# Two places for the first scores, and fewer idle products, in a fused attention and gated MLP kernel

## The chip, the cores and the metric
The kernel runs on one core of a Trainium2 chip. The metric is the device time of one execution in microseconds. The kernel before took 822.72 us (median of 3 runs, 822.22 to 823.4).

PE is the matmul engine, with PEld for its weight loads; DVE, ACT and POOL are the vector, scalar and general engines; SP issues the transfers (DMA). PSUM is the memory into which PE writes, in 8 banks of 512 fp32 columns.

## What is computed
Windowed attention over 8 batches of 8 heads, 576 positions of 64 dims, and then a gated two-layer product over the 4608 tokens:

```python
def _attn_ref(q, k, v):
    B, H, S, D = q.shape                      # 8, 8, 576, 64
    scores = np.matmul(q, k.transpose(0, 1, 3, 2)) / np.sqrt(D)
    rel = pos[:, None] - pos[None, :]
    mask_plain = (rel >= 0) & (rel < 32)
    mask_dil = (rel >= 0) & (rel < 128) & (rel % 4 == 0)    # heads 4 to 7
    scores = np.where(masks, scores, -1e9)
    attn = softmax(scores)
    return np.matmul(attn, v)

def _moe_ref(x, w_in, w_out):                 # x: 4608 x 512, d_ff 2048
    h = x @ w_in
    g = h * (1.0 / (1.0 + np.exp(-1.702 * h)))
    return g @ w_out
```

## The kernel before
Everything is one straight program without loops on the chip. A planner (class `Plan`) takes every step with its cost on each engine that could do it, its urgency, and named keys that it reads and writes. `placed` picks step after step by planned start time and appends it to one order; each engine then runs its own steps in that order, first in, first out. The keys only decide this order. The waits on the chip are put in by the framework from what the instructions really touch.

Two head pairs make a unit: pair k of batch 0 (k = 0 to 3) holds heads 2k and 2k + 1; pairs 2 and 3 are dilated. The text calls the steps of the first batch, "the first entry", s, p and d with the number of the pair:

- s0 to s3, `scores(k)`: a mask product by the identity (line 478) and then 42 tiled products of q and k (line 490, 32 rows of scores each, 64 columns). An fp32 product stands in the trace as two matmuls with two weight loads, hence x84. The result lies in the tile `sp` of two banks, one for each head; there is one such place, key "sp".
- the softmax of k: DVE takes the maximum (line 510) and subtracts it (line 353, pr<-sp) straight out of `sp`; then ACT's exp, DVE's sum and reciprocal, POOL's two multiplications, and DVE's transposes into `ct` (line 695), which has two buffers by turns.
- p0 to p3, `first_product(k)`, line 576: 46 or, dilated, 40 tiled products of v and `ct` into the tile `first_x` of four banks. Pair k takes columns 0 to 143 (k even) or 144 to 287 (k odd) of each bank. The step writes the keys FOUR (acc0 to acc3), all four banks.
- d0 to d3, `drain_x(k)`: ACT copies x into `xs` as the high parts (line 346, xs<-first_x), DVE subtracts to get the low parts (line 353, xs<-first_x,xs), and ACT or DVE copies the last 64 columns (arena<-first_x). These read FOUR, so p of the next pair waits for d of this one.

p0 also waits for s3 (key scores3). Urgency is k - 1e5 for s and p, k for the softmax, 0 for the products of the main block. The main block (class `Group`, `up`, from line 851 on) is x by w_in: for each of 16 columns f four steps c of three 512-column products, step c needing the high and low parts of x for pair c. Then comes the gate (lines 871 and 872), and the second product (lines 800 to 804). Weights arrive packed and are decoded on ACT, DVE and POOL (`decode`, from line 363 on) in the order of use.

Where PE's next step is planned later than PE is free, `placed` fills in idle products (lines 183 to 193), until 60 us of plan and until the third main column begins: `size` is the planned time of one, and a gap gets as many whole ones as fit after 0.5 us is taken off. Before 25 us of plan it may first put in small ones (line 188), just enough to take the count of instructions over the next multiple of 256 after 193. `fetched` is the planner's account of instructions that are loaded in blocks of 256; `count=` of a step is the number of its instructions. The idle products are issued by `warm` (line 1252 on): small ones of 16 columns at line 1262, others of 512 columns at line 1258.

Of the kernel before, what the change touches and what calls it, by code (L numbers as in the profile page):

```python
# [7 lines left out]
F32 = mybir.dt.float32  # L8
# [39 lines left out]
class Plan:  # L48
# [62 lines left out]
    def placed(self, warm_until, soon, late=None):  # L111
# [41 lines left out]
        while any(open_):  # L153
# [28 lines left out]
            cost = abs(ops[i][0][e])  # L182
            if e == PE and when < warm_until:

                at, size = max(free[e], 1.0), 0.26 if when > 8.0 else 0.44
                if when < SHORT and blocks[-1] < when - 0.3:

                    small = min((193 + 256 * (len(blocks) - 1) - issued[0]) // 4 + 1, int((when - at - 0.1) / 0.045))
                    order.extend([(None, e)] * small)
                    at = fetched(4 * small, at, small * 0.045)  # L190
                idle = max(0, int((when - max(at, 1.5) - 0.5) / size))
                fetched(2 * idle, at, idle * size)
                order.extend([(-1, e)] * idle)
            order.append((i, e))
            starts[i] = when
            if e == PE:
# [20 lines left out]
def tile_windowed_attention_then_gated_mlp(  # L217
# [87 lines left out]

    mask, plain = fixed([P, QT, W], BF16, "mask"), fixed([P, QT, W], BF16, "plain")
    ident = fixed([P, P], BF16, "ident")
    ones = fixed([P, 32], F32, "ones")
    V.memset(ones, 1.0)
    for p in sets[0:2]:  # L310
        V.memset(p[:, :, :, W], 1.0e-9)
    V.memset(ident, 1.0)
# [157 lines left out]

    def scores(k):
        u = pairs[k]
        u["sp"] = bank([P, 2, GT], "sp", f"sp_{k}")
        u["all"] = u["sp"][:, :, 0:QT * W].rearrange("p a (t w) -> p a t w", t=QT)
        u["box"] = [u["all"][:, a] for a in range(2)]
        if masked(k):
            for a in range(2):
                T.matmul(u["box"][a], ident, plain if not dilated(k) else classes if k < NC else mask, start=True,
                         stop=False, skip_group_check=True)
        for t in range(QT):  # L480
            for a, g in [(a, g) for a in range(2) for g in range(4 if k < NC or t < QT - 1 else 2)]:
                rows = slice(D * a, D * a + D)
                dst = u["box"][a][32 * g:32 * g + 32, t]
                at = ROW * g + 32 * t if k < NC else HALF * (g // 2) + W * t + 32 * (g % 2)

                spans = [(0, W, at - 32)]
                if at + 32 > S:
                    spans = [(0, S + 32 - at, at - 32), (S + 32 - at, at + 32 - S, 0)]
                for w, n, first in spans:
                    T.matmul(dst[:, w:w + n], u["qk"][rows, at:at + 32], u["qk"][rows, S + first:S + first + n],  # L490
                             start=not masked(k), stop=True, tile_position=(D * a, 32 * g), skip_group_check=True)

    def add_mask(k, urgency):
        u, pr, mine = pairs[k], prs[turn(k)], mask if dilated(k) else plain
        for n, tiles, cost in ((P, slice(0, QT - 1), 0.62), (D, slice(QT - 1, QT), 0.22)):
# [2 lines left out]
                mine[0:n, None, tiles].broadcast_to([n, 2, tiles.stop - tiles.start, W]), ALU.add),  # L498
                ("sp",), (f"pr{turn(k)}",))

    def exponentials(k, urgency):
        u, y = pairs[k], turn(k)
        pr, mx = prs[y], mxs[y]
        PR, MX = f"pr{y}", f"mx{y}"
        held = ("sp",) if masked(k) else ()

        def sp():
            return u["all"] if masked(k) else pr

        add({DVE: 0.80}, urgency, lambda e: V.tensor_reduce(out=mx, in_=sp(), axis=AX.X, op=ALU.max),  # L510
            held or (PR,), (MX,))
        add({DVE: 0.80 if masked(k) else -0.80}, urgency, lambda e: pair(
            e, pr, sp(), mx[:, :, :, None].broadcast_to([P, 2, QT, W]), ALU.subtract), (*held, MX), (PR,))
        add({ACT: 0.75}, urgency, lambda e: A.activation(prs[y], prs[y], AF.Exp, scale=0.125), (), (PR,))
# [98 lines left out]
    def drain_x(k, urgency):  # L613
# [24 lines left out]
                     (GT - HALF, lambda y: y[:, HALF:], lambda: x(1, 0, GT - HALF), 1)]  # L638
            rests = [(lambda y: y, lambda: x(2, 0, LT), 1)]
        if b == 0:  # L640

            if dilated(k):
                mains = [(GT, lambda x: x.rearrange("p (i r) -> p r i", r=4), lambda: u["x"][:, :, 0:P])]
                rests = [(lambda x: x.rearrange("p (i r) -> p r i", r=4), lambda: u["x"][:, :, P:])]
# [3 lines left out]
                rests = [(lambda x: x, lambda: u["x"][:, 3, GT - 3 * ROW:])]  # L648
            for n, (size, part, src) in enumerate(mains):
                add({ACT: 0.12 + size * (0.0019 if dilated(k) else 0.00094)}, urgency, lambda e, part=part, src=src: copy(  # L650
                    e, part(xh[:, c]), src()), FOUR, (f"xh{c}.{n}",))
                add({DVE: 0.08 + size / (490 if dilated(k) else 820)}, urgency, lambda e, part=part, src=src: pair(
                    e, part(xl[:, c]), src(), part(f32(xh[:, c])), ALU.subtract), (*FOUR, f"xh{c}.{n}"), (f"xl{c}.{n}",))
            for n, (part, src) in enumerate(rests):
                add({ACT: 0.22, DVE: 0.2}, urgency, lambda e, part=part, src=src: copy(
                    e, part(rests_x[:, 1, c]), src()), FOUR, (f"xr1{c}.{n}",))
            store_rest(b, c, urgency)
            return
        banks = ("av", "left") if k < INNER else ("sp", "sp")
# [23 lines left out]
    def first_attention(k):  # L683
# [1 line left out]

        load_qk(k)
        load_v(k)
        add({PE: 1.5 if k else 2.3}, k - 1.0e5, lambda e: scores(k), (lots(k)[0],), ("sp", f"scores{k}"), count=180)
        softmax(k, k)

    def first_transposed(k):
# [5 lines left out]
    def first_multiplied(k):  # L697


        y = turn(k)  # L700
        add({PE: 1.4}, k - 1.0e5, lambda e: first_product(k), (lots(k)[1], f"ct{y}.0", f"ct{y}.1", f"scores{NC - 1}"),
            FOUR, count=184)
        drain_x(k, k)

    def attention(k, urgency):
# [547 lines left out]
    def warm(i):  # L1253
        if 2 not in main[0].hps:
            if "idle" not in misc:
                misc["idle"] = bank([P, GT], "av", "idle")
            if i is not None:
                T.matmul(misc["idle"], ident, ident[:, None, :].broadcast_to([P, GT // P, P]), start=True, stop=True)
                return
            n = misc["small"] = misc.get("small", 0) + 1  # L1260
            col = 32 * (n % 4)
# [51 lines left out]
```

## Time and profile before

| | |
|---|---|
| median of 3 runs | 822.72 us |
| span of the profiled execution | 820.7 us |
| difference of the two, around the span | 2.0 us |
| PE busy, share of the span | 809.3 us, 99% |
| DVE, ACT, POOL busy | 669.0, 518.0, 328.4 us |
| chain of work that ended last | PE 97%, DMA 1%, DVE 1% |
| first of the 512-column main products | 25.62 us |
| p3 ends | 32.76 us |

Busy time is the union of an engine's instructions; matmul ends are modelled, so a busy PE is not PE at its peak, and the rate is read from starts. A row of the timeline merges instructions of one kind that follow each other: start, length, engine, line, operation, tiles written <- read, shape, count, and in brackets how long the engine stood idle before and what released it. "issue" there is a wait that no semaphore explains. The granted clock of PE is 1.00 at 2.4 GHz and 0.50 at 1.2 GHz. Ahead of the first change of clock that the profile recorded it prints 1.00 too; there the length of an idle product tells more.

### The profile page before, as it was taken

What the parts mean: (1) busy time and instruction counts of PE and PEld (TensorE: products, weight loads), DVE (VectorE), ACT (ScalarE), POOL (GpSimd) and SP (SyncE); (2) the same over time, 40 slices, a digit from 0 to 9 for tenths busy, and PEclk for the clock granted to TensorE, in tenths of its full rate; (3) what the DMA queues carried; (4) which work ended last, traced back from release to release, by engine and by line L of the source; (5) the groups of instructions that cost most, each with busy time, mean ns of one, the idle gap of its engine ahead of it and who ended that gap; (6) DMA issues with size and microseconds to landing.
All of it is one profiled execution on the core that took longest, in us unless ns stands there. A gap on an engine that the chain in (4) does not pass through costs nothing.

```text
span 820.7 us, 18890 instructions
## 1 busy us (share of the span) xinstructions
PE 809.3 (99%) x7279; PEld 653.4 (80%) x7279; DVE 669.0 (82%) x1081; ACT 518.0 (63%) x988; POOL 328.4 (40%) x294
## 2 busy tenths in 40 slices
PE   7999999999999999999999999999999999999997
PEld 4677878888887888778888888888888888888886
DVE  6898988888888876899889899996679885867575
ACT  7898986767577766786866654545456534544340
POOL 3442325455556553244345445531215332112251
PEclk9999999999999999999999999999999999999999
DMA  9577658899758657797788777775565658674545
GB/s 354 186 249 212 175 161 296 287 318 303 241 176 271 223 180 243 252 307 234 235 236 264 253 254 249 234 256 183 179 207 189 198 189 275 201 226 157 180 153 181
DMA packets 109610, 188.13 MB, mean 229 GB/s; under 512 B 26448, under 2 KB 55376, under 8 KB 109520
## 3 DMA queue, kind: packets, MB, share of 16 engines
q1 hardware_dynamic: 109376, 186.78, 70.2%
q8 instruction: 58, 0.95, 0.5%
q14 instruction: 32, 0.26, 0.1%
q10 hardware_dynamic: 144, 0.13, 0.0%
HBM read 140.64 MB, written 45.09 MB: 226 GB/s over the span
## 4 chain that ended last, share of the span: by engine, by line
PE 97%; DMA 1%; DVE 1%; issue 0%; ACT 0%; SPq 0%; DVEq 0%
PE hp_m L863 16%; PE up_p L1006 10%; PE up_r L1006 9%; PE up_q L1006 9%; PE acc_m L800 5%; PE second_p_Q L1121 5%; PE second_q_Q L1121 5%; PE acc_m L804 5%; PE acc_m L801 5%; PE second_r_Q L1121 5%; PE sp L490 4%; PE second_q_Z L1121 3%; PE second_r_Z L1121 3%; PE second_R L1121 3%; PE second_p_Z L1121 3%; PE av L608 2%
## 5 line engine op out<-in xcount | busy, mean ns | idle before, releaser
L353 POOL TENSOR_TENSOR arena<-arena 128x256 f32<-128x256 f32 (+3 forms) x94 | 100.7, 1083 | 97.8 <-DVE wi_last_units L353 21.6
L863 PE MATMUL hp_m<-xs,wi_kept 128*128 128x512 f32 x504 | 127.7, 396 | 1.2 <-DVE arena L872 0.9
L863 PEld LDWEIGHTS hp_m<-xs,wi_kept 128*128 128x128 f32 x504 | 92.9, 188 | 22.8 <-DVE arena L872 1.9
L353 POOL TENSOR_TENSOR wo_kept<-arena,wo_kept 128x512 fp32r<-128x512 f32 x41 | 56.9, 1395 | 131.5 <-ACT wo_kept L346 84.9
L346 ACT ACTIVATE wo_kept<-arena 128x512 fp32r<-128x512 f32 x111 | 69.2, 630 | 40.7 <-PE second_r_Q L1121 10.9
L1006 PE MATMUL up_r<-wi_kept,xs 128*128 128x512 f32 x336 | 85.3, 389 | 0.0
L1006 PE MATMUL up_p<-wi_kept,xs 128*128 128x512 f32 x336 | 84.2, 394 | 0.2 <-DVE arena L353 0.2
L1006 PE MATMUL up_q<-wi_kept,xs 128*128 128x512 f32 x336 | 83.4, 389 | 0.0
L1006 PEld LDWEIGHTS up_p<-wi_kept,xs 128*128 128x128 f32 x336 | 62.1, 188 | 14.7 <-DVE arena L353 0.9
L1006 PEld LDWEIGHTS up_q<-wi_kept,xs 128*128 128x128 f32 x336 | 63.0, 188 | 13.3 <-DVE arena L1028 0.3
L1006 PEld LDWEIGHTS up_r<-wi_kept,xs 128*128 128x128 f32 x336 | 63.1, 188 | 13.1
L353 DVE TENSOR_TENSOR wo_kept<-arena,wo_kept 128x512 fp32r<-128x512 f32 x80 | 61.1, 775 | 5.1 <-ACT wo_kept L346 4.7
L346 ACT ACTIVATE bt<-ct 32x256 f32<-32x256 f32 (+1 forms) x130 | 56.6, 435 | 11.7 <-DVE ct L534 6.0
L353 POOL TENSOR_TENSOR pr<-pr,sm 128x320 f32<-128x320 f32 x52 | 43.7, 856 | 48.5 <-DVE sm L518 43.5
L800 PE MATMUL acc_m<-gh,wo_kept 128*128 128x512 f32 x156 | 61.5, 394 | 0.0
L353 POOL TENSOR_TENSOR wo_kept<-wi_last_units,wo_kept 128x512 fp32r<-128x512 f32 x22 | 29.9, 1361 | 78.3 <-ACT wo_kept L346 72.3
L353 DVE TENSOR_TENSOR arena<-arena 128x512 f32<-128x512 f32 (+1 forms) x75 | 59.1, 797 | 2.7 <-ACT arena L346 1.8
L801 PE MATMUL acc_m<-gh,wo_kept 128*128 128x512 f32 x156 | 60.8, 390 | 0.0
L1027 ACT ACTIVATE arena<-arena 128x512 f32<-128x512 f32 x60 | 37.4, 628 | 33.4 <-DVE arena L353 27.2
L1028 DVE SCALAR_TENSOR_TENSOR arena<-arena 128x512 f32<-128x512 f32 x60 | 49.8, 837 | 1.7 <-ACT arena L1027 1.3
L346 ACT ACTIVATE gh<-arena 128x512 fp32r<-128x512 f32 x57 | 36.0, 631 | 17.5 <-DVE arena L872 5.8
L353 DVE TENSOR_TENSOR gl<-arena,gh 128x512 fp32r<-128x512 f32 x53 | 41.3, 779 | 6.5 <-ACT gh L346 3.2
(267 smaller groups left out, 1824.7 us busy)
## 6 DMA issues: line engine op xcount, KB each, us to landing
xs<-sums SPq DMA_DIRECT2D x168, 256.0 KB, 3.3
out_weights<-sums_o SPq DMA_DIRECT2D x63, 512.0 KB, 3.5
qk<-qk_dram SPq DMA_DIRECT2D x29, 576.0 KB, 4.4
xs<-sums_o SPq DMA_DIRECT2D x21, 512.0 KB, 3.8
v<-vp_dram SPq DMA_DIRECT2D x28, 320.0 KB, 4.1
sums_o<-arena SPq DMA_DIRECT2D x32, 256.0 KB, 3.2
sums<-arena SPq DMA_DIRECT2D x32, 256.0 KB, 2.9
arena<-wi_dram SPq DMA_DIRECT2D x15, 512.0 KB, 4.7
```

The costliest lines, as they stand in the source:

```text
L346: A.activation(dst, src, AF.Copy, scale=scale)
L353: (V if e == DVE else G).tensor_tensor(out=dst, in0=a, in1=b, op=op)
L490: T.matmul(dst[:, w:w + n], u["qk"][rows, at:at + 32], u["qk"][rows, S + first:S + first + n], start=not masked(k), stop=True, tile_positi ...
L608: T.matmul(u["x"][i][rows, at:at + last - first], u["v"][keys, a, m], bt[keys, m, a, first:last], start=(bank_, a) not in begun, stop=True ...
L800: T.matmul(self.acc[j], w[:, 0, cols], high, start=f == 0, stop=False)
L801: T.matmul(self.acc[j], w[:, 1, cols], high, start=False, stop=False)
L804: T.matmul(self.acc[j], w[:, 0, P * j:P * j + P], low, start=False, stop=f == NF - 1)
L863: T.matmul(hps[f], wi(f)[:, st, cols], mv[:, c], start=c == 0 and k == 0, stop=c == NC - 1 and k == 2)
L1006: T.matmul(self.banks[place], xs[:, slot, at:at + P], wi_kept[:, 2 * a + c, mv], start=fresh and c == 0 and k == 0, stop=c == 1 and k == 2 ...
L1027: add({ACT: 0.60}, -10.0, lambda e: A.activation(unit(tmp), src(), AF.Tanh, scale=0.851), need, own(tmp))
L1028: add({DVE: -0.70 if need[0][0] == "A" else 0.70}, -10.0, lambda e: V.scalar_tensor_tensor(out=unit(dst), in0=unit(tmp), scalar=1.0, in1=s ...
L1121: T.matmul(self.second[key], w[:, st, cols], mv, start=fresh and y == 0 and k == 0, stop=y == 1 and k == 2, skip_group_check=True)
```

## The change
- The scores of pairs 1 and 3 go to columns 192 to 511 of the first two banks of `first_x`; those of 0 and 2 stay in `sp`. Their keys are "x1" and "sp" (`home`).
- The products write the key "x0" or "x1" by turns in place of FOUR, which they now only read; the drains read both. So in the planner p of the next pair no longer waits for d of this one; p1 and p3 wait for the softmax of 3 and for d1.
- Pairs 0 to 3 leave out the second of two spans at the last tile (columns of keys that wrap round): 40 products in place of 42.
- `count` is set to the real numbers: 164 for scores, 184 or 160 for products.
- After 8 us of plan an idle product is now an fp32 one by `wide`, a new 128 x 128 tile of ones, planned at 1.3 us and four instructions; up to 8 us it stays as it was. `wide` is filled by POOL at the start.

```diff
-                at, size = max(free[e], 1.0), 0.26 if when > 8.0 else 0.44
+                at, size, n = max(free[e], 1.0), 0.44, 2
+                if 8.0 < when:
+                    size, n = 1.3, 4
...
-                fetched(2 * idle, at, idle * size)
-                order.extend([(-1, e)] * idle)
+                fetched(n * idle, at, idle * size)
+                order.extend([(-n // 2, e)] * idle)
...
-    ones = fixed([P, 32], F32, "ones")
+    ones, wide = fixed([P, 32], F32, "ones"), fixed([P, P], F32, "wide")
     V.memset(ones, 1.0)
+    G.memset(wide, 1.0)
...
-        u["sp"] = bank([P, 2, GT], "sp", f"sp_{k}")
+        u["sp"] = first_x[:, 0:2, GT - QT * W:] if k in (1, 3) else bank([P, 2, GT], "sp", f"sp_{k}")
...
-                    spans = [(0, S + 32 - at, at - 32), (S + 32 - at, at + 32 - S, 0)]
+                    spans = [(0, S + 32 - at, at - 32)] if k < NC else [
+                        (0, S + 32 - at, at - 32), (S + 32 - at, at + 32 - S, 0)]
...
+    def home(k):
+        return "x1" if k in (1, 3) else "sp"
+
...
-        held = ("sp",) if masked(k) else ()
+        held = (home(k),) if masked(k) else ()
...
+            X = f"x{k % 2}"
...
-                    e, part(xh[:, c]), src()), FOUR, (f"xh{c}.{n}",))
+                    e, part(xh[:, c]), src()), (X, *FOUR), (f"xh{c}.{n}",))
...
-        add({PE: 1.5 if k else 2.3}, k - 1.0e5, lambda e: scores(k), (lots(k)[0],), ("sp", f"scores{k}"), count=180)
+        add({PE: 1.5 if k else 2.3}, k - 1.0e5, lambda e: scores(k), (lots(k)[0],), (home(k), f"scores{k}"), count=164)
...
-        add({PE: 1.4}, k - 1.0e5, lambda e: first_product(k), (lots(k)[1], f"ct{y}.0", f"ct{y}.1", f"scores{NC - 1}"),
-            FOUR, count=184)
+        add({PE: 1.4}, k - 1.0e5, lambda e: first_product(k), (lots(k)[1], f"ct{y}.0", f"ct{y}.1", f"scores{NC - 1}", *FOUR),
+            (f"x{k % 2}",), count=160 if dilated(k) else 184)
...
-                T.matmul(misc["idle"], ident, ident[:, None, :].broadcast_to([P, GT // P, P]), start=True, stop=True)
+                a = ident if i == -1 else wide
+                T.matmul(misc["idle"], a, a[:, None, :].broadcast_to([P, GT // P, P]), start=True, stop=True)
```

## Rows read from the trace of the kernel before

**Rows 1.** The page, busy us of each engine (share of the span, instructions).

```profile
PE 809.3 (99%) x7279; PEld 653.4 (80%) x7279; DVE 669.0 (82%) x1081; ACT 518.0 (63%) x988; POOL 328.4 (40%) x294
```

**Rows 2.** PE's waits (total, times, longest); chain of waits; PE's timeline from 38 us.

```profile
PE hp_m L863 <- DVE arena L872: 0.9, 1, 0.9
...
63.79 2.72 PE hp_m L863 x12
...
37.80 1.99 PE L863 MATMUL hp_m<-xs,wi_kept 128*128 128x512 f32 x5
```

**Rows 3.** PE's timeline from 0 to 60 us.

```profile
13.97 1.13 PE L490 MATMUL sp<-arena 64*32 64x64 f32 x84
15.03 2.33 PE L1258 MATMUL idle<-ident 128*128 128x512 bf16 x10
...
17.56 0.86 PE L490 MATMUL sp<-arena 64*32 64x64 f32 x65
20.25 0.37 PE L490 MATMUL sp<-arena 64*32 64x64 f32 x19 [1.83 <-issue]
20.55 1.49 PE L576 MATMUL first_x<-ct,v 32*64 32x32 f32 x92
21.96 2.63 PE L1258 MATMUL idle<-ident 128*128 128x512 bf16 x6
24.53 1.16 PE L576 MATMUL first_x<-ct,arena 32*64 32x32 f32 x92
25.62 1.65 PE L863 MATMUL hp_m<-xs,wi_kept 128*128 128x512 f32 x6
...
27.43 1.42 PE L576 MATMUL first_x<-ct,arena 32*64 32x64 f32 x80
...
31.68 1.08 PE L576 MATMUL first_x<-ct,arena 32*64 32x64 f32 x80
32.69 7.11 PE L863 MATMUL hp_m<-xs,wi_kept 128*128 128x512 f32 x27
```

**Rows 4.** SP's timeline: the issues of the second qk and of a weight.

```profile
2.19 0.43 SPq L435 DMA_DIRECT2D arena<-qk_dram  x1
...
4.13 0.45 SPq L392 DMA_DIRECT2D bt<-wi_dram  x1
```

**Rows 5.** The same two DMA issues: count, size, us from issue to landing.

```profile
arena<-qk_dram SPq DMA_DIRECT2D x1, 576.0 KB, 7.1
...
bt<-wi_dram SPq DMA_DIRECT2D x1, 512.0 KB, 10.8
```

**Rows 6.** Windows: busy by engine in order of the page, clock, DMA share, GB/s.

```profile
16.00:17.00 1.00, 1.00 (x7) 0.41 (x6) 0.82 (x2) 1.00 (x2) 1.00 (x2) 1.00 1.05 425
22.00:23.00 1.00, 1.00 (x5) 0.39 (x4) 0.92 (x3) 0.91 (x4) 0.01 (x1) 0.50 0.43 157
```

**Rows 7.** DMA queues from 17 to 18 us (packets, MB, share); PEld's timeline.

```profile
q8 instruction: 1, 0.02, 6.9%
...
28.18 0.58 PEld L576 LDWEIGHTS first_x<-ct,arena 32*64 32x64 f32 x41 [0.18 <-issue]
```

**Rows 8.** DVE's and ACT's timelines: maximum and subtraction of s3, drains.

```profile
20.72 0.82 DVE L510 TENSOR_REDUCE mx<-sp 128x10 f32<-128x640 f32 x1 [1.22 <-PE sp L490]
21.58 0.82 DVE L353 TENSOR_TENSOR pr<-sp,mx 128x640 f32<-128x640 f32 x1
22.90 0.76 DVE L353 TENSOR_TENSOR xs<-first_x,xs 128x432 fp32r<-128x432 f32 x2
34.08 0.28 DVE L348 COPY arena<-first_x 128x64 f32<-128x64 f32 x1 [0.94 <-ACT xs L346]
...
22.09 0.66 ACT L346 ACTIVATE xs<-first_x 128x432 fp32r<-128x432 f32 x2 [1.07 <-PE first_x L576]
```

**Rows 9.** DVE's and PE's timelines from 102.5 us: low weights, first main product.

```profile
102.55 0.68 DVE L353 TENSOR_TENSOR wi_kept<-arena,wi_kept 128x512 fp32r<-128x512 f32 x1
...
103.80 0.61 PE L863 MATMUL hp_m<-xs,wi_kept 128*128 128x512 f32 x2
```

More of the change, by code (lines that the diff above doesn't have):

```diff
@@ L650, in drain_x @@
                 add({ACT: 0.12 + size * (0.0019 if dilated(k) else 0.00094)}, urgency, lambda e, part=part, src=src: copy(
-                    e, part(xh[:, c]), src()), FOUR, (f"xh{c}.{n}",))
+                    e, part(xh[:, c]), src()), (X, *FOUR), (f"xh{c}.{n}",))
                 add({DVE: 0.08 + size / (490 if dilated(k) else 820)}, urgency, lambda e, part=part, src=src: pair(
-                    e, part(xl[:, c]), src(), part(f32(xh[:, c])), ALU.subtract), (*FOUR, f"xh{c}.{n}"), (f"xl{c}.{n}",))
+                    e, part(xl[:, c]), src(), part(f32(xh[:, c])), ALU.subtract), (X, *FOUR, f"xh{c}.{n}"), (f"xl{c}.{n}",))
             for n, (part, src) in enumerate(rests):
                 add({ACT: 0.22, DVE: 0.2}, urgency, lambda e, part=part, src=src: copy(
-                    e, part(rests_x[:, 1, c]), src()), FOUR, (f"xr1{c}.{n}",))
+                    e, part(rests_x[:, 1, c]), src()), (X, *FOUR), (f"xr1{c}.{n}",))
             store_rest(b, c, urgency)
```

## The prediction, made before the change was run
> **What bounds the kernel now.** Read the page's busy shares first: PE is busy 809.3 of 820.7 us [rows 1]. Its list of waits then says how little it stands still in the main block: 0.9 us behind line 872, and five products that took 1.99 us near 38 us, some 0.6 us more than their work [rows 2]. So from the first back-to-back main products on, the run is PE work laid end to end, and an edit ahead of that point is worth what it moves that point. Where the point lies is read from PE's timeline [rows 3]. Main products run at 2.72 / 12 = 0.227 us each [rows 2]; 27 of them follow from 32.69 us on, and 12 others (two groups of six like that at 25.62 us) were already done, worth 2.72 us, so the block starts, counted back, at 32.69 - 2.72 = 29.97 us. Ahead of it the order is s0, s1, s2, s3 (scores of the four head pairs), then p0, p1, p2, p3 (their products), each with a drain d0 to d3 by ACT and DVE. The change touches only this stretch.
>
> **What releases the scores early.** In the kernel before, each scores step waits until DVE has subtracted the maximum of the one before out of the same banks. With a second place that wait goes, and the landing of q and k is late next. s1 gains nothing: its qk, issued at 2.19, takes 7.1 us and lands at 9.29 [rows 4, 5]. The qk of s2 lies second of four transfers between 9.29 and 4.13 + 10.8 = 14.93 [rows 4, 5]: by bytes, 9.29 + 5.64 x 1088/2112 = 12.2 us, so s2 starts near 12.2 in place of 13.97 [rows 3]. The qk of s3 follows the transfer that lands at 14.93; 576 KB at the 425 GB/s of that time [rows 6] are 1.4 us: 16.3 us. s3 would end near 17.8 (40 products instead of 42, at about the 1.1 us of s2 [rows 3] or somewhat more) in place of 20.62: 2.8 us earlier.
>
> **The instruction stream.** s3 now stops after 65 of 84 records for 1.83 us, released by nothing ("issue") [rows 3]; a 16 KB packet of the instruction queue moves in that time [rows 7]. Counting matmuls and weight loads over the timeline from the start, the stop is after 2 x 479 = 958 instructions; the next visible break, p2's weight loads, where the last 41 begin at 28.18 after a pause for nothing [rows 7], is after 1470, that is 512 on. So blocks of 256 are fetched, and the edges are 702, 958, 1214, 1470. Crossing 702 (inside s2, near 14.4) to resuming at 20.25 took 5.9 us; from there to 28.18 two more blocks, 4.0 us each [rows 3, 7]. The change cuts 8 instructions from each scores step (two products of two passes, with their loads) and nearly all idle ones: s3 ends at 196 + 92 + 4 x 164 = 944, short of the edge. The stop moves into p0 after 14 instructions. Edge 702 is now crossed near 13.0, so p0 goes on at 13.0 + 5.9 = 18.9 and ends near 20.2, against 22.03 before [rows 3]. p1 meets 1214 in its middle and waits until 18.9 + 4.0 to 5.9 = 22.9 to 24.8; it ends at 23.6 to 25.5 (before: 25.69).
>
> **What the second place costs.** s3 now lies in banks 0 and 1 of the tile that p0 writes, and the two subtracting steps of s3 read there (0.82 us each [rows 8]). The planner keeps X keys by column, but the trace shows bank-wide waits on this very tile: the DVE copy of x at 34.08 us sat idle 0.94 us behind ACT's copy of other columns [rows 8]. So I take p0 and the maximum and subtraction of s3 as serial; before they overlapped (20.55 to 22.03 beside 20.72 to 22.40 [rows 3, 8]). p0 is ready the moment s3 ends, so it is queued first, and everything on DVE behind the maximum waits for p0. For the same reason p1 is queued ahead of d0, since the planner thinks them apart, and ACT stands with d0, and the decode behind it, until p1 is through.
> The Trainium skill (PSUM — Partial Sum Buffer, section on PSUM bank collisions) says the same against this change: any two engines on one bank and quadrant must be kept apart, also at disjoint columns. By column alone p0 would free DVE 1.6 us sooner; the 0.94 us wait sides with the page.
> The chain on that tile, from p0's resuming at 18.9: p0 1.3, maximum and subtraction 1.65, p1 1.3 plus 0.3 to 1.9 of stop, d0 1.6 (22.09 to 23.66 [rows 8]), p2 1.35, d1 1.6, d2 2.7 (p2's end at 28.85 to p3 at 31.68 [rows 3]), p3 1.1 to 1.4. Sum: p3 ends at 31.8 to 34; I take 33.6, since p1 to p3 run at the lower clock (below). Before, 32.76 [rows 3]: **+0.85 us**. The 2.8 us gained on the scores are spent on 1.65 of serial reads, on the stop now in p1, and on drains queued behind products.
>
> **Main products that lose their place.** PE's queue is in order. Before, 12 main products ran ahead of p3, filling waits for d0 to d2 [rows 3]. With p2 and p3 allowed as soon as their own half is drained, and products ranked ahead of main ones, I find room for three (between p2 and p3). Nine fewer at 0.227 us: **+2.05 us**, as p3 then holds the queue until d2 is through. Bounds: no loss if the planner still slips twelve in; 2.7 us if none.
>
> **Idle products and the clock.** They run where PE would stand anyway; their price is that they are too long, and their worth is the clock. At 22 us the granted clock was 0.50 (1.2 GHz) and six idle products took 2.63 us; at 16 us it was 1.00 (2.4 GHz) and ten took 2.33 us [rows 3, 6]. It fell after the stop in s3 and rose again after those six. The new rule fills a gap only from 0.5 + 1.3 = 1.8 us up, and the gaps shrink with the waits, so I expect none to three in place of 29. With only tiled products and stops ahead of them, the main products would start at 1.2 GHz, 0.44 us each by the idle rows in place of 0.23. Bounds: 0 (it has risen) to 3.3 us (some 15 products); I take **+0.8 us**. The long idle product itself is no row: two instructions of 512 columns are 0.46 to 0.9 us by the idle rows, hidden in the gap; if the gap is gone it delays by at most that.
> The Trainium skill (FP8 and Floating Point Precision, TensorE Precision Notes) gives true fp32 four passes; by that such a product would be an estimated 0.9 to 1.8 us.
>
> **Parts at nothing.** Dropped score columns: 2 of 42 products, under 0.1 us a step, hidden behind the qk landings. The new constant's fill is queued on POOL ahead of its first select, in time when POOL stands for DVE; below 0.3 us if not hidden. SP's queue keeps its order; no DMA is added.
>
> **What is given back.** The PE waits behind line 872 (0.9 us, 1.1 counted from product to product) and near 38 us (0.6 us) [rows 2] are waits for gating and decoded weights, not PE work. A later PE meets them ready: up to **-1.7 us**, if ACT and DVE are not late themselves. The sum: 0.85 + 2.05 + 0.8 - 1.7 = +2.0 us. The profiled execution has a span of 820.7 against a median of 822.72 for the runs, so 2.0 us lie around the span and stay: 822.7 + 2.0 = **824.7 us**.
>
> **The rivals.**
> Faster: products and reads of different columns do overlap, or the queue order happens to suit the banks. Then p1 is bound by its stop (ends 24.7), p2 ends near 27, p3 behind edge 1470 (near 28) at 29.3; six main products before it give a start of 29.3 - 1.4 = 27.9 us, 2.0 earlier than 29.97. For it: s3 is ready 2.8 us earlier and the stop leaves it. Against: the 0.94 us wait, and the decode: the weights of one late step were ready at 102.55 + 0.68 = 103.23, used at 103.80 [rows 9], a lead of 0.57 us, so a PE that is 2.0 us early waits unless ACT and DVE win as much from their idle time ahead of the maximum of s3 (DVE, 1.22 us) and of d0 (ACT, 1.07 us) [rows 8]. About 820.8 us.
> Same: the lost places come out at half, the clock is back in time, and the waits given back cover the rest: 822.5 us.
> Much slower: the clock stays at 1.2 GHz well into the block. It decides where p3 stands still long before 32 us with no idle products ahead of it. +0.85 + 2.05 + 2.5, with 0.6 given back: 827.5 us.
>
> **How the numbers follow.** Forecast 0.34, much slower 0.12, same 0.22, faster 0.32. About 0.2% (1.65 us) is what a measurement of this kernel can tell from no change. Faster by over that 0.32, within 0.22, slower 0.46. The range reaches from below the faster case, 820.0, to the much slower, 827.5, leaving out less than 2 in 10; the forecast's own range is 822.9 to 826.5.
>
> **What would show it.** In the changed profile: s3's first record near 16.3 and no "issue" wait inside it; a stop just behind p0's start; the DVE maximum of s3 beginning only after p0's end; ACT's first copy of x waiting for p1; three or so main products ahead of p3; a granted clock of 0.50 at 25 to 32 us. Wrong if the maximum of s3 runs beside p0, if p3 ends before 31 us, or if main products between p0 and p3 number twelve or more.

## The result, and the profile after

The changed kernel took **832.75 us** (median of 4 runs, 831.0 to 834.22; the kernel before beside it 823.06). The ratio is 1.0113, with a 95% interval of 1.0095 to 1.0132: some 9.3 us slower. The prediction said slower, but by 2 us, and its range ended at 827.5.

The profiled execution has a span of 832.5 us against 820.7. PE's busy time has not grown, as the page of after shows against [rows 1]: the loss is time in which PE stands or runs at a low clock.

```profile
PE 807.5 (97%) x7240; PEld 653.2 (78%) x7240; DVE 669.5 (80%) x1075; ACT 515.8 (62%) x996; POOL 322.2 (39%) x293
```

PE's timeline of after from 12 us on answers to [rows 3]. Line 494 is s, 583 is p, 870 the main products, 807 the first of the second products.

```profile
12.15 0.90 PE L494 MATMUL sp<-arena 64*32 64x64 f32 x41 [0.67 <-DMA arena<-qk_dram]
14.62 0.87 PE L494 MATMUL sp<-arena 64*32 64x64 f32 x39 [1.56 <-issue]
...
16.18 1.39 PE L494 MATMUL first_x<-arena 64*32 64x64 f32 x80
17.50 0.43 PE L583 MATMUL first_x<-ct,v 32*64 32x32 f32 x6
20.91 1.54 PE L583 MATMUL first_x<-ct,v 32*64 32x32 f32 x86 [2.98 <-issue]
25.62 1.65 PE L583 MATMUL first_x<-ct,arena 32*64 32x32 f32 x92 [3.17 <-DVE pr L356]
28.03 1.97 PE L870 MATMUL hp_m<-xs,wi_kept 128*128 128x512 f32 x3 [0.75 <-ACT xs L349]
30.99 1.47 PE L583 MATMUL first_x<-ct,arena 32*64 32x64 f32 x80 [0.99 <-ACT arena L406]
33.21 1.65 PE L870 MATMUL hp_m<-xs,wi_kept 128*128 128x512 f32 x3 [0.75 <-ACT xs L349]
35.91 1.48 PE L583 MATMUL first_x<-ct,arena 32*64 32x64 f32 x80 [1.05 <-ACT xs L349]
37.32 8.71 PE L870 MATMUL hp_m<-xs,wi_kept 128*128 128x512 f32 x30
...
46.23 0.50 PE L807 MATMUL acc_m<-gh,wo_kept 128*128 128x512 f32 x1 [0.19 <-ACT gh L349]
```

The scores do come earlier: s3 starts at 16.18 and ends near 17.5. Nothing behind them does. p0 stops after its first records and goes on at 20.91; p1, p2 and p3 start 1.1, 3.6 and 4.2 us later than in [rows 3], and the closing block of main products 4.6 us later, with 6 of them done instead of 12. No idle product of 512 columns was issued at all.

The second products start at 46.23. In the kernel before they start at:

```profile
39.63 0.39 PE L800 MATMUL acc_m<-gh,wo_kept 128*128 128x512 f32 x1
```

That is 6.6 us, and 36 main products lie ahead of this point instead of 39 (3 x 0.227 = 0.7 us more): **the start cost 7.3 us**, against 0.85 + 2.05 + 0.8 = 3.7 in the prediction. The spans differ by 11.8 us, so in this pair of executions **4.5 us more were lost behind the start**, where the prediction had 1.7 us given back. The execution of after that was profiled was the longest of its four (834.22 us); by the 9.3 us of the medians, 2.0 us are left behind the start. PE's list of waits of after (total, times, longest) shows where; against it, the list of before has behind the start only the 0.9 us of [rows 2] and 0.2 us for a weight.

```profile
PE second_r_Q L1128 <- DMA out_weights<-sums_o: 1.3, 1, 1.3
PE up_p L1013 <- ACT arena L349: 1.1, 1, 1.1
...
PE hp_m L870 <- DVE arena L879: 0.6, 2, 0.4
PE acc_m L807 <- ACT gh L349: 0.4, 2, 0.3
PE up_p L1013 <- DVE wi_kept L356: 0.4, 1, 0.4
...
PE second_r_Q L1128 <- DVE arena L1149: 0.2, 1, 0.2
```

These are 4.0 us against 1.1, so 2.9 of the 4.5 us, and the two longest lie at 746 and 365 us, where no step is that the change names. DVE's and ACT's timelines show the start from the other side, against [rows 8]:

```profile
22.49 0.82 DVE L517 TENSOR_REDUCE mx<-first_x 128x10 f32<-128x640 f32 x1 [5.26 <-PE first_x L583]
23.23 0.89 DVE L702 STREAM_TRANSPOSE ct<-pr 128x320 f32<-128x320 f32 x2
24.05 0.79 DVE L533 TENSOR_REDUCE sm<-pr 128x10 f32<-128x650 f32 x1
24.76 0.81 DVE L356 TENSOR_TENSOR pr<-first_x,mx 128x640 f32<-128x640 f32 x1
...
27.32 0.66 ACT L349 ACTIVATE xs<-first_x 128x432 fp32r<-128x432 f32 x2 [6.95 <-PE first_x L583]
```

The maximum of s3 stands 5.26 us at the head of DVE's queue until p0 has ended (20.91 + 1.54 = 22.45), although it reads other columns than p0 writes. Behind it in the queue lie p1's own transposes, a sum, and then the subtraction; p1 waits for that until 25.57, and ACT waits for p1 with d0, 6.95 us.

### The profile page after: what moved, and what is told of

Read it like the earlier page. It is cut to its first block, busy times and chain, and to the rows that moved or that the text cites. A ratio compares the mean times of both kernels' runs of the same rounds, so it can differ in the third digit from the quotient of the medians.

```text
span 832.5 us, 18824 instructions
## 1 busy us (share of the span) xinstructions
PE 807.5 (97%) x7240; PEld 653.2 (78%) x7240; DVE 669.5 (80%) x1075; ACT 515.8 (62%) x996; POOL 322.2 (39%) x293
## 4 chain that ended last, share of the span: by engine, by line
PE 92%; DVE 3%; DMA 2%; ACT 2%; issue 1%; DVEq 0%; ACTq 0%
PE hp_m L870 16%; PE up_p L1013 9%; PE up_q L1013 9%; PE up_r L1013 9%; PE second_p_Q L1128 5%; PE second_q_Q L1128 5%; PE second_r_Q L1128 5%; PE acc_m L807 5%; PE acc_m L808 5%; PE acc_m L811 5%; PE sp L494 3%; PE second_R L1128 3%; PE second_r_Z L1128 3%; PE second_p_Z L1128 3%; PE second_q_Z L1128 3%; PE av L615 2%
## 5 line engine op out<-in xcount | busy, mean ns | idle before, releaser
L870 PE MATMUL hp_m<-xs,wi_kept 128*128 128x512 f32 x504 | 132.1, 404 | 2.2 <-ACT xs L349 1.5
L349 ACT ACTIVATE wo_kept<-arena 128x512 fp32r<-128x512 f32 x116 | 72.4, 630 | 47.5 <-PE second_r_Q L1128 11.8
L356 POOL TENSOR_TENSOR wo_kept<-arena,wo_kept 128x512 fp32r<-128x512 f32 x35 | 48.0, 1380 | 109.7 <-ACT wo_kept L349 78.7
L1013 PEld LDWEIGHTS up_p<-wi_kept,xs 128*128 128x128 f32 x336 | 62.0, 188 | 16.3 <-ACT arena L349 2.0
L356 POOL TENSOR_TENSOR wo_kept<-wi_last_units,wo_kept 128x512 fp32r<-128x512 f32 x26 | 35.7, 1374 | 95.0 <-ACT wo_kept L349 85.3
L356 DVE TENSOR_TENSOR wo_kept<-arena,wo_kept 128x512 fp32r<-128x512 f32 x86 | 67.2, 788 | 6.6 <-ACT wo_kept L349 6.0
L356 DVE TENSOR_TENSOR arena<-arena 128x512 f32<-128x512 f32 (+1 forms) x76 | 57.2, 761 | 2.5 <-DMA arena<-tokens_x 1.3
L349 ACT ACTIVATE wo_kept<-wi_last_units 128x512 fp32r<-128x512 f32 x47 | 29.6, 630 | 28.6 <-PE second_r_Z L1128 7.6
L349 ACT ACTIVATE arena<-av 128x32 f32<-128x32 f32 (+8 forms) x78 | 23.6, 366 | 35.2 <-PE sp L615 27.0
```

What stands on the lines that cost most here:

```text
L349: A.activation(dst, src, AF.Copy, scale=scale)
L356: (V if e == DVE else G).tensor_tensor(out=dst, in0=a, in1=b, op=op)
L870: T.matmul(hps[f], wi(f)[:, st, cols], mv[:, c], start=c == 0 and k == 0, stop=c == NC - 1 and k == 2)
L1013: T.matmul(self.banks[place], xs[:, slot, at:at + P], wi_kept[:, 2 * a + c, mv], start=fresh and c == 0 and k == 0, stop=c == 1 and k == 2 ...
```

## The experiments

Two theories stood at first. A: the loss is the places, that is the serial reads and the drains queued behind the next products (p1 ahead of d0). B: it is the missing idle products and the clock. Each time below is a median; the ratio is to runs of the kernel before on the same chip.

**One half of the change at a time.** e1 is the kernel before with the idle rule alone; e2 the changed kernel with idle products as short as before; e3 the changed kernel with all scores in `sp`; e4 the changed kernel with the products writing FOUR again.

```diff
e2
-                    size, n = 1.3, 4
+                    size, n = 0.26, 2
e3
-        u["sp"] = first_x[:, 0:2, GT - QT * W:] if k in (1, 3) else bank([P, 2, GT], "sp", f"sp_{k}")
+        u["sp"] = bank([P, 2, GT], "sp", f"sp_{k}")
-        return "x1" if k in (1, 3) else "sp"
+        return "sp"
e4
-(lots(k)[1], f"ct{y}.0", f"ct{y}.1", f"scores{NC - 1}", *FOUR), (f"x{k % 2}",)
+(lots(k)[1], f"ct{y}.0", f"ct{y}.1", f"scores{NC - 1}"), (f"x{k % 2}", *FOUR)
```

e1: 

> The kernel before with the new rule for idle products alone (four long fp32 ones come out, in place of 29 of 512 columns). Theory A, the drains of x are queued behind the next products on one tile whose banks are waited for as a whole: p3 still ends near 33 us, 823 to 825 us. Theory B, the missing idle products leave PE at 1.2 GHz: granted clock 0.50 up to about 40 us, 28 of the first main products at 0.43 us, 827 to 831 us.

e2: 

> The changed kernel with the old size of an idle product (0.26 us of plan, 512 columns bf16). Seven come out, four ahead of s2 and three ahead of s3; the order of the rest is that of the changed kernel. Theory A: 829 to 833 us, p3 still ends near 37 us. Theory B: the clock is back before the main products, 823 to 826 us.

e3: 

> The changed kernel with all four scores in the one place sp, as before; the products' keys by turns stay. The planner puts p0 to p3 in a row without a main product between them. Theory A: the drains are still queued behind products, PE stands for d0 and d1 ahead of p2 and p3, 828 to 833 us. If instead the scores' place is what costs (p0 ahead of the maximum of s3 on one tile): 823 to 825 us.

e4: 

> The changed kernel with products that write all four banks' key again, so that p of the next pair waits for d of this one in the plan; the scores' second place stays. Theory A: the main products are back ahead of p3 (18 of them) and p3 ends near 33 us; 822 to 826 us. Theory B, clock: about as the changed kernel, 829 to 833 us. If the scores' place costs: p0 to the end of the subtraction of s3 still in series, 825 to 828 us.

Measured: e1 831.93 us (ratio 1.0103, 1.0088 to 1.0118), e2 832.3 (1.0106, 1.0089 to 1.0123), e3 831.27 (1.0095, 1.0067 to 1.0122), e4 831.97 (1.0107, 1.0092 to 1.0122). Both theories fall in this form: the idle rule alone costs as much as the whole change, and taking out either part of the places gives nothing back. Four different edits with one price pointed to what they have in common: the planner works out the whole order anew. In e1 the second products start at 41.85, 2.2 us late, with 36 main products ahead of them instead of 39 (0.7 us more), so most of its 8.5 us arise behind the start. That the new order of the whole program is what costs is theory C of the next expectations.

**The order held fixed.** In f1 to f4 the planner's result is replaced by a written list, the order that another kernel's planner had found. The list also fixes which engine takes each step, since the planner chooses that too; "order" means both from here on:

```diff
-        order, starts = self.placed(warm_until, soon)
-        for _ in range(ROUNDS):
-            order, starts = self.placed(warm_until, soon, self.latest(starts, SINCE))
+        order = [(None if i == -9 else i, e) for i, e in json.loads(zlib.decompress(base64.b85decode(ORDER)))]
```

f1 is the changed kernel in the order of the kernel before, its 512-column bf16 idle products included. f2 is the kernel before in its own order, without the 29 such idle products behind s1 (its expectation counts 33: four more stand in the list behind the start of the third main column, where `warm` issues none). f3 is the changed kernel with its own order up to 45 us of plan and the old order behind; f4 the kernel before with the opposite.

f1: 

> The changed kernel's work (second place for the scores, dropped columns) issued in exactly the order of the kernel before, its idle products included, so that the planner has no say. Theory A (bank-wide waits on first_x, no more): the maximum of s3 begins behind p0, 1.3 to 1.6 us later than before, 824 to 826 us. Theory C (what costs is the new order of the whole program, 5 us of it behind 45 us): 822 to 825 us. A time near 831 us would speak against both.

f2: 

> The kernel before in its own order without the 33 idle products that stand behind s1 (it leaves out no other work). Theory B: PE stays at 1.2 GHz until the main products have run for some us, 825 to 829 us, and the first main products take 0.43 us each. If the clock is worth nothing: 822 to 824 us. Theory C expects no more than the clock's price, since the order is unchanged: the waits of PE behind 45 us stay near 2 us.

f3: 

> The changed kernel with its own order for all that is planned before 45 us and the order of the kernel before for the rest. Theory C: the start's loss stays (the main block starts 7 us late), but the later waits of PE fall from 6 us to about 2 us: 827 to 830 us. If the later waits come from the late start itself: as the changed kernel, 831 to 834 us.

f4: 

> The kernel before with its own order for all that is planned before 45 us and the order of the changed kernel for the rest. Theory C: the main block starts as before, but PE waits some 4 us more behind 45 us: 825 to 828 us. If the later waits come from the late start: 822 to 824 us.

Measured: f1 824.09 us (1.0013, 1.0003 to 1.0023), f2 824.05 (1.0011, 1.0002 to 1.0021), f3 831.06 (1.0093, 1.0078 to 1.0108), f4 826.15 (1.004, 1.0024 to 1.0056). So the places with all the waits that they bring cost 1.1 us, and the idle products are worth 0.9 us (the interval begins at 0.2, and the second products of f2 start at 39.71, hardly later than 39.63). The new order of the rest costs 3.3 us in f4. f3 costs 7.7 us, but it has the places and lacks the idle products too. It came out above the range of theory C and in that of its rival, by which later waits come from the late start. One wait of f3 lies at the seam of its two orders; for the same tile after waits 0.3 us there and the kernel before not at all:

```profile
57.59 0.50 PE L933 MATMUL acc_m<-gh,wo_kept 128*128 128x512 f32 x1 [1.51 <-ACT gh L475]
```

Why the places gain nothing even in the old order is read in f1, first PE, then DVE and ACT:

```profile
20.25 1.16 PE L710 MATMUL first_x<-ct,v 32*64 32x32 f32 x92
...
24.91 1.28 PE L710 MATMUL first_x<-ct,arena 32*64 32x32 f32 x92 [2.10 <-ACT pr L648]
26.12 2.93 PE L997 MATMUL hp_m<-xs,wi_kept 128*128 128x512 f32 x6
...
21.47 0.82 DVE L644 TENSOR_REDUCE mx<-first_x 128x10 f32<-128x640 f32 x1 [1.75 <-PE first_x L710]
22.33 0.82 DVE L483 TENSOR_TENSOR pr<-first_x,mx 128x640 f32<-128x640 f32 x1
...
23.25 0.66 ACT L476 ACTIVATE xs<-first_x 128x432 fp32r<-128x432 f32 x2 [2.20 <-DVE pr L483]
```

p0 starts 0.3 us earlier than in [rows 3], but the maximum waits for its end, so maximum, subtraction and d0 follow one after another: d0 starts at 23.25, not at 22.09 as in [rows 8]. p1 starts 0.4 us later than before. (The bracket at p1 names ACT's exponential, which ended at 24.64; the low parts of d0, which p1 has to wait for, ended on DVE at 24.81.) The second products of f1 start at 41.21, 1.6 us late, and most of that is the clock: behind the 2.10 us for which PE stood ahead of p1, the granted clock was 0.66 between 25 and 30 us, and six main products took 2.93 us, where [rows 3] has 1.65. So the 1.1 us hold a stretch of low clock besides the waits.

**Would earlier instructions help?** h3 is f1, and h4 the kernel before, with 50 and 58 of the 68 small idle products left out, so that the edge between two instruction blocks that cut s3 moves behind p0 (an earlier edge then comes to lie in s3).

```diff
h3, in the written list (an entry [-9, 0] is a small idle product)
-[-9, 0], 68 times
+[-9, 0], 18 times
```

h3: 

> The places in the order of the kernel before (824.1 us), with 50 of the 68 small idle products left out, so that the third edge between instruction blocks falls behind p0 instead of into the end of s3. If instructions that come late are what keeps p0 from coming forward: p0 starts at 19 us or before instead of 20.25, and the time is 0.5 to 1.5 us below 824.1. If p1 is bound by ACT and DVE's chain instead: p1 stays near 24.9 us and the time at 824.

h4: 

> The kernel before, order and all, with 58 of the 68 small idle products left out: the same shift of the edge behind p0. If the stop of 1.83 us in s3 only hides in front of another wait, p0 and p1 start as before (20.5 and 24.5 us) and the time stays at 823. If the stop is worth what it takes: 821.2 to 822 us.

Measured: h3 825.08 us (1.0023, 1.0012 to 1.0035), h4 825.42 (1.0035, 1.0022 to 1.0048). PE's timeline of h3, then of h4:

```profile
19.46 1.16 PE L709 MATMUL first_x<-ct,v 32*64 32x32 f32 x92
...
24.28 0.70 PE L1392 MATMUL idle<-ident 128*128 128x512 bf16 x2 [2.68 <-issue]
24.91 1.67 PE L709 MATMUL first_x<-ct,arena 32*64 32x32 f32 x92
```

```profile
19.38 1.16 PE L702 MATMUL first_x<-ct,v 32*64 32x32 f32 x92
...
24.34 0.39 PE L1384 MATMUL idle<-ident 128*128 128x512 bf16 x1 [2.62 <-issue]
24.66 1.16 PE L702 MATMUL first_x<-ct,arena 32*64 32x32 f32 x92
```

p0 comes 0.8 and 1.2 us earlier, and the stop only moves to the next edge, into the idle products ahead of p1. p1 starts where it did. So neither kernel is faster when p0 comes earlier: PE goes on behind the next stop no sooner than 24.3 us. In f1, where no such stop shows ahead of p1, the chain through DVE and ACT held p1 to the same 24.91. Both limits seem to lie there at once. Of h3's expectation only p1's place under the second theory came true, and of its two times neither; both times of h4's were missed. That h3 is 0.8 us slower than f1, and h4 2.9 us slower than the kernel before, is not explained; the execution of h4 that was profiled was the shortest of its six (822.89 us, the others 824.57 to 826.29), so its trace doesn't hold that loss.

**The same work in other orders.** g5, g6 and h1 are the kernel before with one number of the planner nudged; h2 is the changed kernel with such a nudge. The steps are those of the kernels they come from, apart from idle products; only the order is found anew (in g6 and h2 only behind 130 us), and with it the engine of some steps. The page of g6 shows 285 instructions on POOL where [rows 1] has 294:

```profile
PE 810.8 (98%) x7279; PEld 652.8 (79%) x7279; DVE 668.1 (81%) x1084; ACT 518.1 (63%) x994; POOL 315.0 (38%) x285
```

What the order proper costs and what the choice of engines isn't separated here.

```diff
g5 and h1
-        add({PE: 1.4}, k - 1.0e5, lambda e: first_product(k), ...
+        add({PE: 1.5}, k - 1.0e5, lambda e: first_product(k), ...
+        add({PE: 1.3}, k - 1.0e5, lambda e: first_product(k), ...
g6 and h2
-ROUNDS, SINCE, CALM, ROOM = 3, 130.0, 8.0, 3.0
+ROUNDS, SINCE, CALM, ROOM = 3, 130.0, 8.0, 3.1
```

g5: 

> The kernel before, with one number of the planner's costs changed (a first product's cost 1.5 instead of 1.4): the same instructions, written in another order all through. If replanning alone costs time, 825 to 832 us although no work is changed; if the order is neutral as long as the start is nearly the same, 822 to 823.5 us.

g6: 

> The kernel before, with the planner's room 3.1 instead of 3.0, which changes the written order only behind 130 us. If any replanning of the rest costs what the rest's new order cost (3 us): 824 to 827 us. If the order of the rest is neutral by itself: 822.5 to 823.5 us.

h1: 

> The kernel before with the planner's cost of a first product at 1.3 instead of 1.4: the same work in another order. If most new orders cost some microseconds against the order of the kernel before, whatever the nudge: 826 to 833 us, as 832.6 and 827.6 us of the other two. If those two were chance: 823 us.

h2: 

> The changed kernel with the planner's room at 3.1 instead of 3.0, which rewrites its order only late. If the order of the rest is a draw with a spread of some microseconds: a time 1 to 5 us away from 832.75 us, on either side (the start stays at its own cost, so not under 828). If the rest's order is neutral: 832.5 to 833 us.

Measured: g5 832.62 us (1.0116, 1.0097 to 1.0136), g6 827.61 (1.0052, 1.0035 to 1.0068), h1 829.39 (1.0082, 1.0065 to 1.01), h2 835.06 (1.015, 1.0132 to 1.0167). A nudge that changes no step of the work costs up to as much as the change itself. PE's waits of g5, then of g6, that the kernel before has not or has shorter (0.9 us behind line 872 [rows 2]):

```profile
PE hp_m L863 <- DVE arena L872: 4.7, 5, 1.6
...
PE up_q L1006 <- DVE arena L1028: 0.8, 1, 0.8
```

```profile
PE second_p_Q L1121 <- DMA out_weights<-sums_o: 1.6, 1, 1.6
...
PE up_q L1006 <- DVE arena L353: 0.8, 2, 0.5
```

They are of the same kind as those of after: gates, decoded weights and late transfers that an order has put a little too late. In g5 the start is 1.5 us late (second products at 41.11) and the rest some 7 us.

**What in the start's new order costs.** g3 is e4 in its own order up to 45 us with the old rest; as its products wait for d in the plan, more main products stand ahead of p2 and p3. g4 is f3 with 12 short idle products where PE stood. i1 is f3 with p1's transposes and the sum moved ahead of the maximum of s3 on DVE. i2 is i1 with d0 ahead of p1 and two decode steps behind d0. Each is one more written list.

g3: 

> The changed kernel with its second place for scores, but with the products p writing all four columns at once as before, in its own planned order up to 45 us and in the order of the kernel before behind that. The theory that the start's cost (about +7.9 us of the whole) is mostly the order in which p1 to p3 stand ahead of the main products: 825 to 828 us, because this plan lets main products stand ahead of p3 as before. The rival, that the places themselves and the clock cost the start: 830 to 832 us as with the new start.

g4: 

> The new order of the start and the old order of the rest (which took 831.1 us together), with 12 idle products of bf16 added where TensorE stood: 6 behind p0, 1 behind p1, 2 behind the first three main products, 1 behind p2 and 2 behind the next three. If the low clock up to 40.8 us is the main part of the start's cost: the clock rises before 30 us and the time falls to 828 to 830 us. If the order of the stalls sets it whatever the clock: 830.5 to 832 us.

i1: 

> The new start with the old rest (831.1 us), with one move on DVE: the two transposes for p1 and a sum are issued ahead of the maximum of s3, which there stood 5.0 us at the head of DVE's queue until p0 ended. If that queue is a cause: the subtraction of s3 ends 1.5 us earlier (25.3 to 23.8 us), p1 starts near 24.0 instead of 25.34, and the time falls by 1 to 1.6 us. If p1 waits for something else: p1 near 25.3 and 831 us.

i2: 

> The same with p1 issued behind the copies d0 (which then start as p0 and the subtraction end, 24 us, instead of 27.0), and two decode steps of DVE behind them: the exponential of s3 and the later decode steps on ACT, which queue behind d0, then come some 3 us earlier. If p1 ahead of d0 is the main part of the start's cost: 825 to 828 us. If the low clock and the main products' places carry it: 829 to 831 us.

Measured: g3 827.33 us (1.0047, 1.0031 to 1.0064), g4 830.7 (1.0088, 1.0072 to 1.0105), i1 830.38 (1.0089, 1.0074 to 1.0104), i2 830.56 (1.0088, 1.007 to 1.0105); f3 had 1.0093. p0 as it goes on after its stop, and the closing block of main products, in f3 and then in g4:

```profile
20.62 1.55 PE L709 MATMUL first_x<-ct,v 32*64 32x32 f32 x86 [2.58 <-issue]
...
37.02 8.60 PE L996 MATMUL hp_m<-xs,wi_kept 128*128 128x512 f32 x30
```

```profile
19.56 1.54 PE L710 MATMUL first_x<-ct,v 32*64 32x32 f32 x86 [1.46 <-issue]
...
35.35 7.20 PE L997 MATMUL hp_m<-xs,wi_kept 128*128 128x512 f32 x30
...
PE up_p L1140 <- DMA xs<-sums: 1.7, 1, 1.7
```

In g4 the block starts 1.7 us earlier and runs 1.4 us shorter, as the clock has risen by 35 us (0.57 from 30 to 35 us, 1.00 from 35 us on): the start is some 2.3 us better (second products at 43.51 instead of 45.81). Of the 1.7 us, 1.1 are there when p0 goes on, ahead of the first of the added idle products, so they can't be put down to these. The time is no better: the intervals overlap, and a later wait of 1.7 us has come up that f3 has not. i1 shows a better start without a better time as well, on DVE and PE:

```profile
21.70 0.82 DVE L643 TENSOR_REDUCE mx<-first_x 128x10 f32<-128x640 f32 x1 [2.85 <-PE first_x L709]
22.56 0.83 DVE L482 TENSOR_TENSOR pr<-first_x,mx 128x640 f32<-128x640 f32 x1
...
23.44 0.97 PE L709 MATMUL first_x<-ct,arena 32*64 32x32 f32 x42 [1.78 <-DVE pr L482]
24.81 1.03 PE L709 MATMUL first_x<-ct,arena 32*64 32x64 f32 x50 [0.41 <-issue]
```

p1 starts 1.9 us earlier than in f3, of which p0 brings 0.5 (it goes on at 20.11), so DVE's queue was a cause of p1's lateness; a part goes again to an instruction stop in the middle of p1, the second products start 1.3 us earlier, and the time falls by less than its interval. In i2 d0 starts at 23.72 on ACT, 3.3 us earlier than in f3, and p1 only at 25.61. Its block starts 2.0 us earlier than f3's (34.97) but takes 9.41 us, with the granted clock at 0.50 from 35 to 40 us, and the time stays. The theory that p1 ahead of d0 carries the start's cost falls. g3, whose plan lets six main products run ahead of p2 and twelve more ahead of p3, is the only new start that wins clearly, 3 us and more of f3's 7.7; it differs from f3 in more than this, so which of its moves wins isn't shown. g4, i1 and i2 bring the second products forward by 1.3 to 2.3 us and change the time by 0.4 to 0.7 us, within the intervals. So the start's cost is made up of several waits, each worth 1 to 2.5 us at the start, and what one is worth in the whole can't be read off the start, since later waits take most of it back. Which order of the start would win it all is open. Two real tiles for x, one for each half, were not tried.

## Why the prediction was off, step by step

**s1 to s3 earlier: right.** s2 was put at 12.2 and starts at 12.15; s3 at 16.3 and starts at 16.18; its end was put at 17.8 and is 17.5.

**The instruction stream: mechanism right, size wrong.** The stop left s3 and lies in p0, as said. But the resuming was put at 18.9 and is 20.91. The failing term is the crossing of edge 702 "near 13.0": in the trace of after PE stops there too, 1.56 us, and goes on at 14.62. One more block, 6.3 us by the two rows, is 20.91. That the stops are late instructions shows in the transfers of after: 16 KB packets of the instruction queue start at 5.84, 12.05 and 18.33 us and take 0.9 to 1.1 us, and PE goes on 1.5 us behind the end of each (8.29, 14.62, 20.91). Eight of the kernels have one PE order up to p0 (after, e4, f3, g3, g4, h2, i1, i2); in them p0 goes on between 19.30 and 21.18, 6.0 to 6.3 us after PE goes on in s2. So the 5.9 us put for a block was near, and the size of the miss differs by up to 1.9 us from one execution to the next. In the other kernels with a stop here, p0 or s3 goes on between 18.96 and 20.77; making the scores earlier does not bring the instructions earlier.

**Serial reads: right, undersized.** The maximum begins at 22.49, behind p0's end at 22.45. For maximum and subtraction 1.65 us were put; from p0's end to the subtraction's end it is 25.57 - 22.45 = 3.1 us, since the planner, which thinks the maximum runs beside p0, put p1's transposes and a sum between the two. The text had said that everything on DVE behind the maximum waits for p0, and priced none of it. f1 prices these waits in the old order: 1.1 us in all, with the low clock behind them. The rows agree with the page of the Trainium skill that was weighed there (PSUM — Partial Sum Buffer, section on PSUM bank collisions), by which two engines on one bank and quadrant are to be kept apart also at disjoint columns: PE and DVE took turns, and DVE waited 5.26 us. The turns are semaphore waits that the framework put in, so no run shows a collision, nor whether the wait goes by bank or by the whole tile.

**The chain to p3: 33.6 put, 37.39 measured.** 2.0 us come from p0's resuming, 1.5 from DVE's queue, and 1.0 from p2 (30.99, [0.99 <-ACT arena L406]). The bracket names a decode step of ACT, but that ended at 30.62, and the second transpose that p2 reads ended later, at 30.78, on DVE:

```profile
30.28 0.50 DVE L702 STREAM_TRANSPOSE ct<-pr 128x320 f32<-128x320 f32 x1
```

It stood there behind the low parts of d0 and the sum of s3, so p2's lateness is DVE's queue again. Put against this, p1 met no stop.

**Lost places: too many.** Six main products ran ahead of p3's end, not three: 1.4 us lost instead of 2.05.

**The clock: the rival's mechanism.** No idle product was issued, as expected, and the low clock lasted well into the block, as the much slower rival had it. PE's timeline of after, in two narrow windows:

```profile
37.32 2.93 PE L870 MATMUL hp_m<-xs,wi_kept 128*128 128x512 f32 x6
...
41.32 2.45 PE L870 MATMUL hp_m<-xs,wi_kept 128*128 128x512 f32 x10
```

Six products take 2.93 us at 37 us and ten take 2.45 us at 41 us, behind the first rise of the granted clock that is recorded, at 40.78 us. Until the second products the block of 30 takes 8.9 us where 30 x 0.227 is 6.8: 2.1 us, against +0.8 put (2.5 in the rival). That rival's 827.5 was still 5 us short, since it held the other terms as they were. Chain, places and clock come to 4.6 + 1.4 + 2.1 = 8.1 us; the 0.7 us by which the block of the kernel before was longer than its 27 products [rows 2, 3] are not there in after, which leaves the 7.3 us of the start.

**Given back: wrong in sign, and the main failure.** The step said that a later PE meets its gates and weights ready. It rests on the sentence "The change touches only this stretch". It does not: keys, costs and counts feed one planner, and the order of all 800 us came out anew. The wait near 38 us (0.6 put, 0.7 found) was given back, and a part of that behind line 872 (0.6 us in after, line 879), but new waits came up for gates, weights and transfers. Behind the start 2.0 us (by the medians) to 4.5 us (by the profiled pair) were lost; f4 shows 3.3 us of such a loss with the old start. So the term was off by 4 to 6 us, as much as or more than the three terms of the start missed together (3.7 put, 7.3 us measured). And the kernel before stands on an order that is hard to meet: three nudges without any work behind them cost some 4, 7 and 10 us. The chance of faster (0.32) was far too high for that reason.

So of the 9.3 us, the experiments show some 1 us for the places themselves and some 1 us for the idle products, both in the old order, and the rest for a new order. f3's 7.7 us hold these two, and the 1.5 us at the seam; by subtraction some 4 us are left for the order of the start, beside the 3.3 us of the rest in f4. No run measures these 4 us alone. Why the order of the kernel before is better than each of the four others of its work that were measured (g5, g6, h1, f4) isn't settled.

## What to carry to other kernels

Where a planner orders the whole program, an edit's price is for the most part that of its new order, and a nudged planner on the unchanged kernel measures the spread of that price: in three nudges here 4 to 10 us, larger than any term of the sum. Hold the order fixed to learn what an edit is worth by itself, and only then let the planner have it. A buffer that the planner takes for two and the waits on the chip take for one makes an engine's queue stand behind its own head.

## What was not expected of the hardware

An idle product of fp32 costs as e1's timeline shows, at the low clock and then at the high one:

```profile
10.77 2.07 PE L1262 MATMUL idle<-wide 128*128 128x512 f32 x2
...
14.32 1.98 PE L1262 MATMUL idle<-wide 128*128 128x512 f32 x4
```

Two records make one product. At 10.77 one takes 1.94 us to the next product; behind a rise of the granted clock at 13.2 us the four records start at 14.32, 14.85, 15.28 and 15.71, so one takes 0.86 us once it runs. The prediction had taken two runs of 512 columns for it, 0.46 to 0.9 us by the rows of bf16, which is half. The Trainium skill (FP8 and Floating Point Precision, TensorE Precision Notes) gives fp32 four passes, and the estimate of 0.9 to 1.8 us that followed from it fits at the high clock and is a little low at the low one. Blocks of 256 instructions came 6.3 us apart in after (PE goes on at 8.29, 14.62 and 20.91) in a stretch in which all transfers moved 406 to 416 GB/s (5 to 20 us), where 4.0 us apart were seen later in the kernel before [rows 7].
